# Gate and value of a gated feed-forward layer: plain products in 512-token blocks, and Strassen's seven products of halves

## The chip, the cores and the metric

The kernel runs on one core of a Trainium2 chip. The metric is the device time of one execution in microseconds (us). The engines named below are TensorE (PE in the rows; PEld is its weight load), VectorE (DVE), ScalarE (ACT), GpSimd (POOL) and SyncE (SP), which issues every transfer here. SBUF is the on-chip memory of 128 partitions, PSUM the eight accumulator banks of 128 x 512 fp32 into which TensorE writes, DRAM the memory off the core.

## The reference

```python
# attention: 4 batches, 8 heads, 576 tokens, head 64, causal window 128
x = attention(q, k, v)                 # 2304 tokens x 512
h = np.maximum(x @ w_in, 0)            # moe1: 512 -> 2048
x = (h * h) @ w_out                    #       2048 -> 512
gate = 1 / (1 + np.exp(-(x @ w_gate))) # moe2: 512 -> 1536
val  = x @ w_val                       #       512 -> 1536
out  = (gate * val) @ w_out2           #       1536 -> 512
```

The weights arrive as 64-bit floats. All matrix products are of fp32 accuracy.

## The kernel before

Each weight tile of 128 x 512 is read from DRAM as 64-bit words, turned into fp32 by one operation of ScalarE and four of VectorE (`weight`, L422 to L432), and split into a rounded high part `wh` and the remainder `wl` (the copy at L335, the subtraction at L332). Activations are split likewise. A product then takes three matmuls: high by high, high by low, low by high.

The program has three stages that overlap. Attention and moe1 go through 8 chunks of 256 or 320 tokens; an H step is one of the 16 column tiles of `w_in`, a Y step the matching row tile of `w_out`, and attention for later chunks is laid between the steps. moe1's result goes to DRAM (`yscr`). moe2 works in one block of 256 tokens and four of 512. For each of twelve column tiles `f`, `gv` makes gate and value, each in one PSUM bank (`pg`, `pv`) by 4 x 3 matmuls over the four 128-row pieces of the contraction (L885 to L887), with no break on the bank. Then ScalarE takes the sigmoid (L896), VectorE multiplies (L898), and the product is split into `asp` (`asp5` in the blocks of 512; L335, L332). One tile later `o_step` adds it onto the four output banks, three matmuls of 512 columns each (L915 to L917).

The order of the instructions on every engine is fixed when the program is built. `op` records an operation with the engines that may do it, its keys read and written, and a priority; `Plan.schedule` then replays the program with a cost for each operation (VectorE's is `dve_ns`, L37: 68 + n/0.96 ns for n elements) and lets each engine take the ready operation of lowest priority whose buffers fit. `GROUP` says from which group of SBUF or PSUM slots a buffer comes, `SIZE` how many a group has, `CAP` how many of a kind may be held at once. moe2's weights are loaded, unpacked and split beside the end of moe1 and the first block (`WB`), and stay in SBUF.

Of the kernel before, what the change touches and what calls it, by code (L numbers as in the profile page):

```python
# [287 lines left out]
def attention_moe_moe2_kernel(ctx: ExitStack, tc, q, k, v, w_in, w_out1, w_gate, w_val, w_out2, out):  # L288
# [169 lines left out]
    def attend(u, due, long):  # L458
# [13 lines left out]
        for src, t0, nt, a0 in ((q, u.q0, nq, 0), (k, u.k0, nk, 2 * nq)):
            a = t0 * 128
            r = min(128, (S - a) // nt)
            if pq:
                t = turned[a0] = new("nq" if a0 == 0 else "nk", [128, nt, 2, 64], F32, early)
                op({"SP": 630}, lambda e, t=t, src=src, a=a, nt=nt, r=r: nc.sync.dma_start(
                    out=t()[0:r], in_=src[u.b, h0:h0 + 2, a:a + r * nt, :].rearrange("h (p j) d -> p j h d", j=nt)),
                   w=[t], prio=pl, data=364 * nt)
                continue  # L480

            def load(e, src=src, nt=nt, a0=a0, a=a, r=r):
                nc.sync.dma_start(
                    out=nat()[0:r, a0:a0 + 2 * nt].rearrange("p (h j) d -> p h (j d)", h=2),
                    in_=src[u.b, h0:h0 + 2, a:a + r * nt, :].rearrange("h (p j) d -> p h (j d)", j=nt))

            op({"SP": 475}, load, w=[(nat, a0)], prio=pl, data=182 * nt)
# [24 lines left out]
        if pq:  # L512

            qs, ks = new("qs", [128, 256], F32, early), new("ks", [128, 384], F32, early)
            parts = ((qs, nq, vq, 0), (ks, nk, vk, 2 * nq))
            banks = [new("tq", [128, 512], F32, early)] * 2 if kind == "c" else [new(kd, [128, 512], F32, early) for kd in ("tq", "tk")]
            c0s = (0, nqc if kind == "c" else 0)

            def turn(e, which):
                for z in which:  # L520
                    _, nt, v_, a0 = parts[z]
                    for j in range(nt):
                        nc.tensor.transpose(banks[z]()[:, c0s[z] + j * v_:c0s[z] + (j + 1) * v_],
                                            turned[a0]()[0:v_, j].rearrange("p h d -> p (h d)"), C["ident"][0:v_, 0:v_])

            def place(e, z):
                dst, nt, v_, _ = parts[z]
                nc.scalar.activation(
                    out=in_order(dst()[:, :nt * v_], nt), in_=by_tile(banks[z]()[:, c0s[z]:c0s[z] + nt * v_], nt), func=AF.Copy,
                    scale=C["qmul"][:, u.hp:u.hp + 1] if z == 0 else 1.0)  # L530

            for which in ((0, 1),) if kind == "c" else ((0,), (1,)):
                op({"PE": sum(parts[z][1] * 2 * pe_ns(parts[z][2]) for z in which) + (60 if kind == "c" else 0)},
                   lambda e, which=which: turn(e, which), cols=.5, r=[turned[parts[z][3]] for z in which],
                   w=[banks[which[0]]], prio=p(1 + which[0] / 2), also=[parts[z][0] for z in which])
            for z in range(2):
                op({"ACT": act_ns(parts[z][1] * parts[z][2], True) + (94 if z == 0 else 0)}, lambda e, z=z: place(e, z),
                   r=[banks[z]], w=[parts[z][0]], prio=p(1.3 + z / 2))
        else:

            qkn = new("qkn", [128, 10, 2, 64], F32R)
            op({"ACT": act_ns(64 * n)}, copy(lambda: qkn()[:, :n, 0], lambda: nat()[:, :n]), r=qkkeys, w=[(qkn, 0)], prio=p(0))
            op(dve_or_pool(64 * n), minus(lambda: qkn()[:, :n, 1], lambda: nat()[:, :n], lambda: qkn()[:, :n, 0]),
               r=qkkeys + [(qkn, 0)], w=[(qkn, 1)], prio=p(0), port=True)
            qs, qw = new("qs", [128, 2, 256], F32R, early), new("qw", [128, 2, 256], F32R, early)
            if kind == "b":
                ks = [new("ks", [128, 384], F32R, early) for i in range(2)]
                kof = lambda i, c0, c1: ks[i]()[:, c0:c1]
            else:
                ks = [new("ks", [128, 2, 256], F32R, early)] * 2  # L550
                kof = lambda i, c0, c1: ks[i]()[:, i, c0:c1]

            def turn(what, prio, also):
                banks = [new(kd, [128, 512], F32, early) for kd, _, _ in what]

                def go(e):
                    for ps, (_, rows, v) in zip(banks, what):
                        for z, t in enumerate(rows):
                            nc.tensor.transpose(ps()[:, z * v:(z + 1) * v].bitcast(F32R),
                                                qkn()[0:v, t].rearrange("p x d -> p (x d)"), C["identr"][0:v, 0:v])  # L560

                op({"PE": sum(len(rows) * pe_ns(v) for _, rows, v in what) + 54}, go, r=[(qkn, 0), (qkn, 1)], w=banks, prio=prio, also=also)
                return banks

            whole = ("tq", range(2 * nq), 128)
            if kind == "b":
                ps, = turn([whole], p(1), [qs, qw])
                kps = turn([("tk", range(2 * nq + i * nk, 2 * nq + (i + 1) * nk), 128) for i in range(2)], p(2), ks)
            else:
                ps, kps = turn([whole, ("tk", range(2 * nq, n), 128)], p(1), [qs, qw, ks[0]])  # L570
            for i in range(2):
                op({"ACT": act_ns(nqc, True)}, copy(
                    lambda i=i: in_order(qs()[:, i, :nqc], nq), lambda i=i, ps=ps: by_tile(ps()[:, i * nqc:(i + 1) * nqc], nq),
                    qmul[h0 + i]), r=[ps], w=[(qs, i)], prio=p(1.5))
            for i in range(2):
                r_, o_ = slice(64 * i, 64 * i + 64), slice(64 - 64 * i, 128 - 64 * i)
                def swap(e, r_=r_, o_=o_):
                    if e == "ACT":
                        nc.scalar.activation(out=qw()[o_, :, :nqc], in_=qs()[r_, :, :nqc], func=AF.Copy)
                    else:  # L580
                        nc.vector.tensor_copy(qw()[o_, :, :nqc], qs()[r_, :, :nqc])

                op({"DVE": dve_ns(2 * nqc, True)}, swap, r=[(qs, 0), (qs, 1)], w=[(qw, i)], prio=p(2), port=True)
            if kind == "b":
                for i in range(2):
                    op({"ACT": act_ns(nkc, True)}, copy(
                        lambda i=i: in_order(ks[i]()[:, :nkc], nk), lambda i=i: by_tile(kps[i]()[:, :nkc], nk)),
                       r=[kps[i]], w=[(ks[i], i)], prio=p(2))
            else:
                op({"ACT": act_ns(2 * nkc, True)}, copy(  # L590
                    lambda: ks[0]()[:, :, :nkc].rearrange("c h (p j) -> c h j p", j=nk),
                    lambda: kps()[:, :2 * nkc].rearrange("c (h j p) -> c h j p", h=2, j=nk)),
                   r=[kps], w=[(ks[0], 0), (ks[0], 1)], prio=p(2))
# [434 lines left out]
```

## Time and profile before

| what | us |
|---|---|
| median of 3 runs (1014.94 to 1016.01) | 1015.13 |
| the profiled execution | 1015.93 |
| its span, first to last instruction | 1014.2 |
| TensorE busy | 1002.9 |
| ScalarE busy | 462.9 |
| VectorE busy | 442.9 |
| GpSimd busy | 107.9 |

The profile is of one execution and gives each instruction's start and duration. Matmuls are pipelined, so the duration of one is longer than its distance from the next; the distance is the price of a matmul in a row of them. A busy TensorE is not one at its peak. The granted clock is given in parts of full speed.

### The profile page before, as it was taken

To read this page: it belongs to the slowest core of one execution; us is meant where nothing else is said; L and a number is where in the kernel's file an instruction comes from. 1 tells how busy PE (TensorE), PEld (TensorE's weight loads), DVE (VectorE), ACT (ScalarE), POOL (GpSimd) and SP (SyncE) were. 2 spreads that over 40 slices of the span, in tenths; PEclk is the share of its full clock that TensorE was granted. 3 is DMA by queue.
4 is the path that set the end of the run, shared out by engine and by line. 5 is a ranking of instruction groups with operands and counts; after the bars stand their busy time and mean duration, and the time that the engine had idled before them with its cause. 6 is when DMAs were issued, how large, how long until landed. Compare 5 with 4: busy or idle time off the path is not lost.

```text
span 1014.2 us, 16829 instructions
## 1 busy us (share of the span) xinstructions
PE 1002.9 (99%) x6308; PEld 875.0 (86%) x6308; DVE 442.9 (44%) x1248; ACT 462.9 (46%) x1235; POOL 107.9 (11%) x224
## 2 busy tenths in 40 slices
PE   8999999999999999999999999999999999999998
PEld 6699999998998988998999998888888888888886
DVE  6999963344244243246799972112211221111112
ACT  7887875566555465556677552111211221112111
POOL 3513121122021021021000110000000000000000
PEclk9999999999999999999999999999999999999999
DMA  8556562022312113111455540001100110001001
GB/s 229 136 166 181 161 183 56 21 53 53 86 30 55 31 39 71 35 45 42 138 157 167 171 146 22 1 11 32 42 1 10 32 42 1 1 1 42 0 1 42
DMA packets 112594, 69.26 MB, mean 68 GB/s; under 512 B 79488, under 2 KB 104576, under 8 KB 112512
## 3 DMA queue, kind: packets, MB, share of 16 engines
q1 hardware_dynamic: 112512, 68.18, 23.9%
q8 instruction: 50, 0.82, 0.3%
q14 instruction: 32, 0.26, 0.1%
HBM read 58.72 MB, written 9.44 MB: 67 GB/s over the span
## 4 chain that ended last, share of the span: by engine, by line
PE 89%; ACT 3%; DVE 3%; DMA 3%; issue 1%; SPq 0%; ACTq 0%
PE y L811 18%; PE h L774 6%; PE h L776 6%; PE h L775 6%; PE pg L886 5%; PE pv L886 5%; PE o L915 5%; PE pv L887 5%; PE pg L885 5%; PE pv L885 5%; PE o L917 5%; PE o L916 5%; PE pg L887 5%; PE tv L752 3%; PE ts L614 2%; DMA raw<-in_moe_w_in_dram 2%
## 5 line engine op out<-in xcount | busy, mean ns | idle before, releaser
L811 PE MATMUL y<-gs,wh 128*128 128x256 f32 (+1 forms) x1024 | 216.6, 303 | 0.5 <-DVE gs L332 0.4
L811 PEld LDWEIGHTS y<-gs,wh 128*128 128x128 f32 x1024 | 163.1, 189 | 12.1 <-issue 9.3
L898 DVE TENSOR_TENSOR a<-pv,a 128x512 f32<-128x512 f32 (+1 forms) x60 | 38.3, 638 | 292.2 <-PE pv L887 290.9
L774 PE MATMUL h<-x,wh 128*128 128x256 f32 (+1 forms) x512 | 157.6, 308 | 0.4 <-DVE r L786 0.4
L811 PE MATMUL y<-gs,wl 128*128 128x256 f32 (+1 forms) x512 | 151.2, 295 | 0.0
L776 PE MATMUL h<-x,wl 128*128 128x256 f32 (+1 forms) x512 | 151.2, 295 | 0.0
L775 PE MATMUL h<-x,wh 128*128 128x256 f32 (+1 forms) x512 | 151.1, 295 | 0.0
L896 ACT ACTIVATE a<-pg 128x512 f32<-128x512 f32 (+1 forms) x60 | 33.3, 555 | 189.0 <-PE pg L887 188.8
L332 DVE TENSOR_TENSOR gs<-r,gs 128x320 fp32r<-128x320 f32 (+1 forms) x121 | 56.5, 467 | 137.6 <-ACT gs L335 137.0
L774 PEld LDWEIGHTS h<-x,wh 128*128 128x128 f32 x512 | 97.2, 190 | 5.0 <-issue 3.2
L335 ACT ACTIVATE asp<-a 128x512 fp32r<-128x512 f32 (+1 forms) x60 | 35.3, 589 | 144.1 <-DVE a L898 144.0
L775 PEld LDWEIGHTS h<-x,wh 128*128 128x128 f32 x512 | 96.8, 189 | 0.0
L811 PEld LDWEIGHTS y<-gs,wl 128*128 128x128 f32 x512 | 96.6, 189 | 0.0
L776 PEld LDWEIGHTS h<-x,wl 128*128 128x128 f32 x512 | 96.4, 188 | 0.0
L887 PE MATMUL pv<-x,wl 128*128 128x512 f32 (+1 forms) x240 | 89.2, 372 | 0.0
L885 PE MATMUL pv<-x,wh 128*128 128x512 f32 (+1 forms) x240 | 89.1, 371 | 0.0
L885 PE MATMUL pg<-x,wh 128*128 128x512 f32 (+1 forms) x240 | 89.1, 371 | 0.0
L887 PE MATMUL pg<-x,wl 128*128 128x512 f32 (+1 forms) x240 | 89.1, 371 | 0.0
L729 POOL TENSOR_SCALAR_AFFINE_SELECT pt<-pt 128x256 f32<-128x256 f32 (+1 forms) x144 | 65.1, 474 | 223.1 <-ACT pt L723 206.8
L788 ACT ACTIVATE r<-h 128x256 f32<-128x256 f32 (+1 forms) x128 | 51.8, 406 | 78.9 <-PE h L776 75.7
L915 PE MATMUL o<-wh,asp 128*128 128x512 f32 x216 | 85.2, 395 | 0.0
L917 PE MATMUL o<-wh,asp 128*128 128x512 f32 x216 | 85.2, 394 | 0.0
(105 smaller groups left out, 1763.0 us busy)
## 6 DMA issues: line engine op xcount, KB each, us to landing
raw<-in_moe_w_out_dram SPq DMA_DIRECT2D x28, 512.0 KB, 3.6
raw<-in_moe_w_in_dram SPq DMA_DIRECT2D x16, 512.0 KB, 4.8
raw<-in_moe_w_gate_dram SPq DMA_DIRECT2D x12, 512.0 KB, 3.6
raw<-in_moe_w_val_dram SPq DMA_DIRECT2D x12, 512.0 KB, 3.6
ysg<-yscr SPq DMA_DIRECT2D x18, 256.0 KB, 2.7
out_dram<-ob SPq DMA_DIRECT2D x18, 256.0 KB, 2.0
nq<-in_q_dram SPq DMA_DIRECT2D x32, 128.0 KB, 3.0
yscr<-ys SPq DMA_DIRECT2D x32, 128.0 KB, 1.8
```

What stands on the lines that cost most here:

```text
L332: return lambda e: eng(e).tensor_tensor(out=out(), in0=a(), in1=b(), op=ALU.subtract)
L729: op({"POOL": pool_sel(2 * cols)}, lambda e: nc.gpsimd.affine_select(out=pt_of(what, j), in_=pt_of("own", j), pattern=[[0, 2], [1 if mine ...
L774: nc.tensor.matmul(ps()[:, :N], w[0]()[:, c], x()[:, 0, cc, :N], start=cc == 0, stop=False)
L775: nc.tensor.matmul(ps()[:, :N], w[0]()[:, c], x()[:, 1, cc, :N], start=False, stop=False)
L776: nc.tensor.matmul(ps()[:, :N], w[1]()[:, c], x()[:, 0, cc, :N], start=False, stop=cc == CC - 1)
L788: op({"ACT": act_ns(N, True)}, lambda e: nc.scalar.activation(out=g()[:, :N], in_=ps()[:, :N], func=AF.Relu), r=[ps], w=[g], prio=ep, also ...
L811: nc.tensor.matmul(y()[:, c0:c0 + N], w[a]()[:, c], gs()[:, b, :N], start=f == 0 and p == 0 and n != 1, stop=f == F1 - 1 and p == 2, skip_ ...
L885: nc.tensor.matmul(ps()[:, :NB], w[0]()[:, c], x(0, cc), start=cc == 0, stop=False)
L886: nc.tensor.matmul(ps()[:, :NB], w[0]()[:, c], x(1, cc), start=False, stop=False)
L887: nc.tensor.matmul(ps()[:, :NB], w[1]()[:, c], x(0, cc), start=False, stop=cc == CC - 1)
L915: nc.tensor.matmul(o(), asp()[:, 0, c], w[0](), start=f == 0, stop=False)
L917: nc.tensor.matmul(o(), asp()[:, 1, c], w[0](), start=False, stop=f == F2 - 1)
```

## The change

Gate and value in the four blocks of 512 tokens are made by Strassen's scheme. For a pair of column tiles `f`, `f + 1` of one kind, the weight is a 2 x 2 arrangement of halves (rows of the contraction by column tiles), and so is the block (halves of the tokens by halves of the contraction). Instead of eight products of halves there are seven, P1 to P7, of sums and differences of halves, each of 2 x 3 matmuls of 256 columns. A unit (one kind, one pair) uses two PSUM banks, `pa` and `pd`. P1 goes onto `pa` and ScalarE copies it out; P6, P5 and P3 are added onto the same bank, with copies between. P2 goes onto `pd`, VectorE adds it to a copy; P7 restarts `pd`, VectorE adds that, and P4 is added onto it. The output tiles, four quarters each, come together in SBUF buffers `cg`. `ORDER` spreads the seven products and the four output steps over a unit by priority.

```diff
+    ORDER = ["P1", "P2", "o0", "P6", "o1", "P7", "P5", "o2", "P3", "o3", "P4"]
+    at_unit = {u: 3.0 * i / len(ORDER) for i, u in enumerate(ORDER)}
+    def gv_strassen(n, kind, f, e0):
+        (gh, gl), (_, v2), (t2, t3, t1, t4) = W[kind, f], W[kind, f + 1], TW.pop((n, kind, f))
+        pa, pd = new("pa", [128, 512], F32), new("pd", [128, 512], F32)
...
+            op({"PE": 6 * pe_ns(256)}, go, r=wk + [(bh, ih), (bl, il)] + ([] if start else [ps]), w=[ps], prio=e0 + at_unit[name])
...
+        product("P1", pa, True)
+        product("P2", pd, True)
+        keep(0, 0, pr)
+        add(0, 0, pr)
+        product("P6", pa, False)
+        product("P7", pd, True)
+        keep(0, 1, pr)
+        product("P5", pa, False)
+        keep(1, 1, pr)
+        add(1, 1, pr)
+        product("P3", pa, False)
+        product("P4", pd, False)
+        add(0, 1, pr)
```

`keep` is a copy of 256 columns by ScalarE, `add` an addition of 256 columns by VectorE. For a gate unit three sigmoids follow (256, 256 and 512 elements), for a value unit three multiplications by the gate and two splits. `xb` makes the seven operands of a block's tokens: four quarters are loaded, four sums or differences made, and seven splits.

The weights' operands are made once. During moe1, from chunk 2 to the beginning of chunk 7, `prepare` loads the two tiles of a pair, unpacks them, forms four differences of halves (`tt`), splits all, and stores four pieces of 512 KB in DRAM (`wscr`); `prepare_out` does the same without differences for each output tile. `weight2` reads the plain split weights back once, and `sums` reads the four split differences (`st2`) of a unit in every block.

```diff
+    first, last = begin[2], begin[NC - 1]
+    for f in range(0, F2, 2):
+        jobs += [(prepare, "gate", f), (prepare, "val", f), (prepare_out, f), (prepare_out, f + 1)]
+    for i, (fn, *a) in enumerate(jobs):
+        fn(*a, first + (last - first) * (i + 1) / len(jobs))
...
+            weight2(kind, f, endA + j * 0.7 - 18)
...
+                sums(n, kind, f0, e1 - 9)
+                gv_strassen(n, kind, f0, e1)
...
+    def put(u, p, k, prio):
+        op({"SP": 475}, lambda e: nc.sync.dma_start(
+            out=scr(u, k, 2).rearrange("(k p) c -> p k c", p=128), in_=p().bitcast(F32)),
...
+        for i, x, y, rk in ((1, B[12], B[11], [tg, tw]), (3, B[22], B[12], [tw]), (2, B[22], at_t[1], [tw, (tb, 1)]), (4, B[21], at_t[2], [tg, (ta, 2)])):
+            op(dve_or_pool(256), minus(at_t[i], x, y), r=rk, w=[(tb if i in (1, 4) else ta, i)], prio=prio + .5, port=True)
...
-    CAP = {"raw": 3, "nat": 2, "nq": 2, "nk": 2, "qs": 1, "qw": 1, "ks": 1, "wt": 6, "vs": 3, "st": 4, "pt": 2, "t": 3,
-           "h": 2, "y": 4, "pg": 2, "pv": 2, "o": 4, "ob": 4, "ob5": 2, "ysg": 2, "a5": 2, "asp5": 2}
+    CAP = {"raw": 3, "nq": 1, "nk": 1, "qs": 1, "ks": 1, "wt": 6, "vs": 3, "st": 4, "pt": 2, "t": 3,
+           "h": 2, "y": 4, "pg": 2, "pv": 2, "o": 4, "pa": 2, "pd": 2, "ob": 2, "ysg": 2, "raw2": 2, "pp": 1, "xp": 2,
+           "tg": 1, "tw": 1, "tt": 2, "st2": 6, "xf": 6, "cg": 4, "ah": 3, "al": 3}
...
-    o_step(*prev, endA + 3.0 * F2 * nblk)
+    o_step(nblk - 1, F2 - 2, endA + 3.0 * F2 * nblk, False)
+    o_step(nblk - 1, F2 - 1, endA + 3.0 * F2 * nblk, False)
```

The queries and keys of an attention unit now have one buffer each (`nq`, `nk`), and a branch of attention that was never taken is gone. Since both tiles of a pair come at once, the output step for a tile is recorded two tiles later instead of one, and those of the last pair both at the end.

How the order on the engines moves is shown at three places. First TensorE in a block of 512 tokens, before: the end of a value tile and the beginning of the output step; `pv` is the value's bank, `o` an output bank, `x` and `xs` the tokens, a number tells one buffer from another, and the brackets name the engines for which an instruction waits.

```order
L885 MATMUL pv_9976<-x_9365,wh_6789 128x512
L886 MATMUL pv_9976<-xs_9407,wh_6789 128x512
L887 MATMUL pv_9976<-x_9365,wl_6800 128x512
L915 MATMUL o_9995<-wh_6711,asp5_9951 128x512 [waits Activation_49]
L916 MATMUL o_9995<-wl_6723,asp5_9951 128x512
L917 MATMUL o_9995<-wh_6711,asp5_9951 128x512 [waits Pool_49]
L915 MATMUL o_10000<-wh_6711,asp5_9951 128x512 [waits DVE_49]
L916 MATMUL o_10000<-wl_6723,asp5_9951 128x512
```

And after, within a pair of units, where L936 is the product of `gv_strassen` and L1030 to L1032 the output step; `pa_10350` and `pd_10360` are the gate's two banks, `pa_10370` one of the value's, `st2` and `ah`, `al` the differences and the split result.

```order
L936 MATMUL pa_10370<-x_9473,wl_7924 128x256
L936 MATMUL pa_10350<-x_9473,st2_10262 128x256 [waits DMAHW4_49,Activation_49]
L936 MATMUL pa_10350<-x_9500,st2_10262 128x256
L936 MATMUL pa_10350<-x_9473,st2_10262 128x256 x2
L936 MATMUL pa_10350<-x_9500,st2_10262 128x256
L936 MATMUL pa_10350<-x_9473,st2_10262 128x256
L936 MATMUL pd_10360<-x_9500,st2_10292 128x256 [waits DMAHW5_49,DVE_49]
L936 MATMUL pd_10360<-x_9500,st2_10292 128x256 x5
L1030 MATMUL o_9765<-wh_7823,ah_10378 128x512 [waits Activation_49]
L1031 MATMUL o_9765<-wl_7826,ah_10378 128x512
L1032 MATMUL o_9765<-wh_7823,al_10388 128x512 [waits DVE_49]
L1030 MATMUL o_9771<-wh_7823,ah_10378 128x512
```

Where twelve matmuls of 512 columns stood on one bank without a wait inside, P6 and P7 of the gate now stand between two pieces of other banks, and each waits for the reading of its bank and for a load.

Second, TensorE at the end of the program, before, where `asp5_10402` and `asp5_10446` are the split results of the last two tiles; twelve matmuls of the first stand between the last value product and the first of the second.

```order
L886 MATMUL pv_10424<-xs_9407,wh_8103 128x512
L887 MATMUL pv_10424<-x_9365,wl_8109 128x512
L915 MATMUL o_9995<-wh_8021,asp5_10402 128x512 [waits Activation_49]
L916 MATMUL o_9995<-wl_8032,asp5_10402 128x512
L917 MATMUL o_9995<-wh_8021,asp5_10402 128x512 [waits DVE_49]
L915 MATMUL o_10000<-wh_8021,asp5_10402 128x512
...
L915 MATMUL o_9995<-wh_8161,asp5_10446 128x512 [waits Activation_49]
L916 MATMUL o_9995<-wl_8166,asp5_10446 128x512
L917 MATMUL o_9995<-wh_8161,asp5_10446 128x512 [waits DVE_49]
```

And after, where `ah_12479`, `al_12483` and `ah_12481`, `al_12485` are the two results of the last pair.

```order
L936 MATMUL pd_12419<-xp_11585,st2_12383 128x256 [waits DMAHW7_49,DVE_49]
L936 MATMUL pd_12419<-xp_11585,st2_12383 128x256 x5
L1030 MATMUL o_11744<-wh_7943,ah_12479 128x512 [waits Activation_49]
L1031 MATMUL o_11744<-wl_7953,ah_12479 128x512
L1032 MATMUL o_11744<-wh_7943,al_12483 128x512 [waits DVE_49]
L1030 MATMUL o_11744<-wh_8056,ah_12481 128x512 [waits Activation_49]
L1031 MATMUL o_11744<-wl_8063,ah_12481 128x512
L1032 MATMUL o_11744<-wh_8056,al_12485 128x512 [waits DVE_49]
L1030 MATMUL o_11750<-wh_7943,ah_12479 128x512
```

No matmul is left between the last product, P4 on `pd_12419`, and the output step that needs its result; 24 matmuls follow.

Third, VectorE in moe1, beside an H step (`r`, `gs`) and an attention unit (`ts`, `st`, `sm`), before:

```order
L668 RECIPROCAL sm<-sm 128x2
L676 TENSOR_TENSOR st<-st,sm 128x256
L666 TENSOR_SCALAR sm<-sm 128x2
L668 RECIPROCAL sm<-sm 128x2
L825 COPY ys<-y 128x256
L332 TENSOR_TENSOR gs<-r,gs 128x320
L786 TENSOR_TENSOR r<-h,r 128x320
L332 TENSOR_TENSOR gs<-r,gs 128x320
L641 COPY_PREDICATED ts<-msk,ts 128x2x128 x2
L653 ISA st,sm<-ts,rel 128x128
L653 ISA sm 128x1
```

And after, where `tw` and `tg` are the two weight tiles of a pair that are unpacked and `tt` their differences:

```order
L838 COPY ys<-y 128x256
L467 SCALAR_TENSOR_TENSOR tw<-raw_4176,tw 128x512
L679 TENSOR_SCALAR sm<-sm 128x2
L799 TENSOR_TENSOR r<-h,r 128x320
L681 RECIPROCAL sm<-sm 128x2
L666 ISA st,sm<-ts,rel 128x128
L666 ISA sm 128x1
L335 TENSOR_TENSOR tt<-tw,tg 128x256
L799 TENSOR_TENSOR r<-h,r 128x320
L335 TENSOR_TENSOR tt<-tw,tt 128x256
L335 TENSOR_TENSOR gs<-r,gs 128x320
```

Between the same instructions of moe1 and attention there are now a merge of an unpacked weight (L467) and differences of halves (L335 with `tt`).

## Rows read from the trace of the kernel before

**Rows 1.** The page: busy time, the chain's shares; and the view of cores.

```profile
PE 1002.9 (99%) x6308; PEld 875.0 (86%) x6308; DVE 442.9 (44%) x1248; ACT 462.9 (46%) x1235; POOL 107.9 (11%) x224
...
PE 89%; ACT 3%; DVE 3%; DMA 3%; issue 1%; SPq 0%; ACTq 0%
...
core 0: 1014.2 us, clock 0.997
```

**Rows 2.** Waits of TensorE: total us, times, longest; all eight.

```profile
PE warm L984 <- DVE identr L379: 1.8, 1, 1.8
PE tq L523 <- DMA nq<-in_q_dram: 1.5, 1, 1.5
PE tp L719 <- POOL st L676: 1.5, 2, 1.2
PE tp L719 <- ACT st L674: 0.9, 1, 0.9
PE ts L614 <- ACT ks L528: 0.8, 1, 0.8
PE h L774 <- DVE r L786: 0.4, 1, 0.4
PE y L811 <- DVE gs L332: 0.4, 1, 0.4
PE tk L523 <- ACT ks L528: 0.2, 1, 0.2
```

**Rows 3.** Windows: stretch, its us, PE PEld DVE ACT POOL, PEclk, DMA, GB/s.

```profile
25.00:100.00 75.00, 71.68 (x582) 63.09 (x579) 71.56 (x223) 60.56 (x186) 26.57 (x35) 0.98 0.58 164
180.00:500.00 320.00, 320.00 (x2440) 288.07 (x2439) 129.43 (x499) 186.73 (x574) 44.92 (x122) 1.00 0.20 50
500.00:560.00 60.00, 60.00 (x413) 59.98 (x412) 56.30 (x108) 44.27 (x91) 2.75 (x2) 1.00 0.57 177
...
800.00:900.00 100.00, 100.00 (x432) 80.94 (x431) 19.62 (x29) 18.00 (x30) 1.29 (x1) 1.00 0.04 16
```

**Rows 4.** Timeline of TensorE, block of 256 tokens: start, us, instruction.

```profile
556.87 0.28 PE L885 MATMUL pg<-x,wh 128*128 128x256 f32 x1
...
562.90 0.28 PE L885 MATMUL pv<-x,wh 128*128 128x256 f32 x1
...
564.32 0.39 PE L915 MATMUL o<-wh,asp 128*128 128x512 f32 x1
...
565.71 0.28 PE L885 MATMUL pg<-x,wh 128*128 128x256 f32 x1
...
568.53 0.39 PE L915 MATMUL o<-wh,asp 128*128 128x512 f32 x1
```

**Rows 5.** Timeline, a tile of a 512-token block; brackets: idle before, releaser.

```profile
701.40 0.39 PE L885 MATMUL pv<-x,wh 128*128 128x512 f32 x1
701.61 0.60 ACT L896 ACTIVATE a<-pg 128x512 f32<-128x512 f32 x1 [4.16 <-PE pg L887]
704.19 0.39 PE L915 MATMUL o<-wh,asp 128*128 128x512 f32 x1
704.45 0.69 DVE L898 TENSOR_TENSOR a<-pv,a 128x512 f32<-128x512 f32 x1 [6.28 <-PE pv L887]
705.18 0.63 ACT L335 ACTIVATE asp<-a 128x512 fp32r<-128x512 f32 x1 [2.98 <-DVE a L898]
```

**Rows 6.** Groups, shapes apart: count, busy us, ns of one, idle before.

```profile
L429 DVE SCALAR_TENSOR_TENSOR wt<-raw,wt 128x512 int32<-128x512 int32 x68 | 49.8, 734 | 0.6
L432 DVE SCALAR_TENSOR_TENSOR wt<-raw,wt 128x512 int32<-128x512 int32 x68 | 46.7, 691 | 0.2
L332 DVE TENSOR_TENSOR wl<-wt,wh 128x512 fp32r<-128x512 f32 x56 | 38.5, 695 | 3.4 <-ACT wh L335 3.2
L332 DVE TENSOR_TENSOR asp<-a,asp 128x512 fp32r<-128x512 f32 x46 | 31.9, 692 | 30.8 <-ACT asp L335 30.8
L426 DVE TENSOR_SCALAR wt<-wt 128x512 int32<-128x512 int32 x68 | 29.7, 437 | 0.6
L424 DVE TENSOR_SCALAR wt<-wt 128x512 f32<-128x512 f32 x68 | 29.2, 430 | 7.0 <-ACT wt L422 7.0
L898 DVE TENSOR_TENSOR a<-pv,a 128x256 f32<-128x256 f32 x12 | 5.1, 424 | 6.1 <-PE pv L887 4.8 <-ACT wh L335 0.8 <-issue 0.5
L896 ACT ACTIVATE a<-pg 128x256 f32<-128x256 f32 x12 | 4.6, 384 | 6.7 <-PE pg L887 6.6
```

**Rows 7.** The page, DMA issues: count, KB each, median us to landing.

```profile
ysg<-yscr SPq DMA_DIRECT2D x18, 256.0 KB, 2.7
```

**Rows 8.** Timeline, the last matmul of the program.

```profile
1010.08 0.39 PE L917 MATMUL o<-wh,asp 128*128 128x512 f32 x1
```

More of the change, by code (lines that the diff above doesn't have):

```diff
@@ new lines, in fetch, with weight2 @@
+    def fetch(kind, u, k, prio, after=()):
+        b = new(kind, [128, 512], F32R)
+        b.late = True
+        op({"SP": 475}, lambda e: nc.sync.dma_start(out=b().bitcast(F32), in_=scr(u, k)), r=[("scr", u, k)] + list(after), w=[b], prio=prio, data=728)
+        return b
+    def weight2(kind, f, prio):
+        if kind == "out2":
+            W[kind, f] = fetch("wh", (kind, f), GH, prio), fetch("wl", (kind, f), GL, prio)
+        elif f % 2 == 0:
+            W[kind, f] = fetch("wh", (kind, f), GH, prio), fetch("wl", (kind, f), GL, prio)
+        else:
+            W[kind, f] = fetch("v1", (kind, f - 1), V1, prio), fetch("v2", (kind, f - 1), V2, prio)
@@ L474, in attend @@
             r = min(128, (S - a) // nt)
[L475 to L487, printed above, removed]
+            t = turned[a0] = new("nq" if a0 == 0 else "nk", [128, nt, 2, 64], F32, early)
+            op({"SP": 630}, lambda e, t=t, src=src, a=a, nt=nt, r=r: nc.sync.dma_start(
+                out=t()[0:r], in_=src[u.b, h0:h0 + 2, a:a + r * nt, :].rearrange("h (p j) d -> p j h d", j=nt)),
+               w=[t], prio=pl, data=364 * nt)
         a = u.k0 * 128
@@ L507, in attend @@
             vkeys += [(vn, "v", "pad"), (vn, "v", 2)]
-        qkkeys = [(nat, 0), (nat, 2 * nq)]
         vq, vk = (128, 128) if kind != "c" else (S - 512, (S - 384) // 2)
         nqc, nkc = nq * vq, nk * vk
[L512 to L593, printed above, removed]
@@ new lines, in attend, with turn @@
+        qs, ks = new("qs", [128, 256], F32, early), new("ks", [128, 384], F32, early)
+        parts = ((qs, nq, vq, 0), (ks, nk, vk, 2 * nq))
+        banks = [new("tq", [128, 512], F32, early)] * 2 if kind == "c" else [new(kd, [128, 512], F32, early) for kd in ("tq", "tk")]
+        c0s = (0, nqc if kind == "c" else 0)
+        def turn(e, which):
+            for z in which:
+                _, nt, v_, a0 = parts[z]
+                for j in range(nt):
+                    nc.tensor.transpose(banks[z]()[:, c0s[z] + j * v_:c0s[z] + (j + 1) * v_],
+                                        turned[a0]()[0:v_, j].rearrange("p h d -> p (h d)"), C["ident"][0:v_, 0:v_])
@@ new lines, in place @@
+        def place(e, z):
+            dst, nt, v_, _ = parts[z]
+            nc.scalar.activation(
+                out=in_order(dst()[:, :nt * v_], nt), in_=by_tile(banks[z]()[:, c0s[z]:c0s[z] + nt * v_], nt), func=AF.Copy,
+                scale=C["qmul"][:, u.hp:u.hp + 1] if z == 0 else 1.0)
+        for which in ((0, 1),) if kind == "c" else ((0,), (1,)):
+            op({"PE": sum(parts[z][1] * 2 * pe_ns(parts[z][2]) for z in which) + (60 if kind == "c" else 0)},
+               lambda e, which=which: turn(e, which), cols=.5, r=[turned[parts[z][3]] for z in which],
+               w=[banks[which[0]]], prio=p(1 + which[0] / 2), also=[parts[z][0] for z in which])
@@ L596, in attend @@
+        for z in range(2):
+            op({"ACT": act_ns(parts[z][1] * parts[z][2], True) + (94 if z == 0 else 0)}, lambda e, z=z: place(e, z),
+               r=[banks[z]], w=[parts[z][0]], prio=p(1.3 + z / 2))
         st = new("st", [128, 4, 128], F32, early)
```

284 lines of the change are left out of this document (208 added, 76 removed).

## The prediction

> **What bounds the kernel now.** I read the page's busy times first, then the list of waits, then stretches of 50 to 100 us, and last single instructions. TensorE is busy 99% of the span, at a mean granted clock of 0.997, the upper level of 2.4 GHz, and 89% of the chain that ended last is TensorE [rows 1]. Busy time alone does not show that it works at its pace, so I looked at what it waited for: eight waits in the whole run, 1.8 us the longest, 7.4 us together [rows 2]. In moe2 there is no idle time, and the pace is steady: a 512-token block of 432 matmuls takes 100 us, 0.2315 us per matmul of 512 columns [rows 3]. There VectorE and ScalarE are busy 20% and 18%. So in moe2 only TensorE counts, and time is to be had by giving it fewer columns. In moe1, from 180 to 500 us, VectorE is busy 129 of 320 us; from 500 to 560 us, where moe2's weights are unpacked, 56 of 60, and TensorE has no idle time there [rows 3].
>
> **What goes on TensorE.** A block has twelve column tiles each of gate and value, 24 x 12 matmuls of 512 columns, and 144 for the output. After the change two tiles of one kind and two halves of the tokens are seven products of six matmuls of 256 columns: 12 x 7 x 6 = 504 per block, and the 144 stay. The price of a 256-column matmul with a weight load of its own is in the trace, in the block of 256 tokens: 24 of them from 565.71 to 568.53 us, 0.1175 us each; the twelve from 562.90 to 564.32 us, at 0.1183, are the dearer end; six of 512 columns between took 1.39 us [rows 4]. I take 0.1178. New block: 504 x 0.1178 + 144 x 0.2315 = 59.4 + 33.3 = 92.7 us. Old: 432 x 0.2315 = 100.0 us. That is 7.3 us per block and 29.1 us for four; with 0.1183 it is 28.2, with 0.1175 it is 29.8. The first block keeps its products.
>
> **Hand-overs inside a unit, new.** A unit of seven products now uses two PSUM banks, and five of the products are added onto a bank that ScalarE or VectorE must read first. Nothing in the old trace waits like this, so I bound it. Chain for ScalarE: it starts 0.21 us after TensorE's next slot (701.40 to 701.61) [rows 5], copies 256 columns in 0.384 us [rows 6], and a follower on another engine starts 0.04 us after an end (705.14 to 705.18) [rows 5]: 0.64 us. For VectorE 0.26 + 0.424 + 0.04 = 0.72 us [rows 5, 6]. In the new order of TensorE at least two other pieces (a product, 6 x 0.1178 = 0.71 us, or three output matmuls, 0.69 us) stand between a product and the next on its bank, 1.4 us of cover, because gate's and value's units are interleaved and the output step is spread over them. So each hand-over has some 0.7 us to spare: one 512-element instruction in front (0.63 on ScalarE, 0.69 on VectorE [rows 6]) eats it and a second one doesn't fit. Load on these engines in a pair of units, 14 x 0.707 + 8 x 0.695 = 15.5 us of TensorE: on VectorE nine to ten operations of 256 or 512 elements, about 5.4 us; on ScalarE about 5.0 us; at a block's start 7 splits and 4 sums more. Two queues a third full seldom have two long jobs in front. Bounds: 0, and 0.3 us at a tenth of 240 hand-overs, 7 us; I take 0, the value of the output's own hand-over in the old moe2, which never waited.
>
> **The end, new.** Before, the last output step but one covers the hand-over of the last gate and value. After the change both units of the last pair end together, and all 24 remaining output matmuls need their result. From TensorE's last product [rows 5, 6]: 0.26, add 0.424, 0.04, multiplication 0.69, 0.04, rounding copy 0.63, 0.04: 2.1 us idle; the third matmul waits for the low half (0.04 + 0.69, less two matmuls of 0.23), 0.3 us more. +2.4 us. What follows the start of the last matmul, at 1010.08 [rows 8], keeps its 1014.2 - 1010.08 = 4.1 us.
>
> **Weights from DRAM.** The sums of weights are read again for every block: 48 x 256 KB = 12.6 MB per 92.7 us, 136 GB/s. From 500 to 560 us the queues moved 177 GB/s at a share of 0.57 [rows 3], so this is a share of 0.44. A 256 KB load landed in 2.7 us [rows 7]; in the new order each such load goes into a buffer that is freed at least 12 us of TensorE's work before the load's first use. The reads of the split weights for the first block (72 of 256 KB, 18.9 MB) replace 36 of 512 KB, and each stands over 50 us of TensorE's work ahead. Hidden: 0. What it costs if that cover is gone is rival 3.
>
> **Preparation, moved and added.** 36 tiles are unpacked during chunks 2 to 6 instead of beside chunk 7 and the first block. VectorE, for each a clamp, a shift and two merges: 36 x (0.430 + 0.437 + 0.734 + 0.691) = 82.5 us, 60 splits x 0.695 = 41.7, and 48 differences of 256 elements x 0.424 = 20.4, by the nearest row, a multiplication of that size [rows 6]: 145 us. Some of the last two kinds go to GpSimd; its durations for them stand in no row, so I count all on VectorE. (129 + 145)/320 = 86% of VectorE in a stretch where attention also runs. What it takes away after 500 us gains nothing, as no wait stands there. DMA gets 31.5 MB of writes and 18.9 MB of reads: 157 GB/s over 320 us on top of 50 at a share of 0.20 [rows 3], to about 0.7; q and k of a unit now have one buffer, so their loads start later, but a unit of attention is due eight steps of twelve matmuls (8 x 12 x 0.1178, 11 us and more) before its chunk. Bounds for the new waits: from 500 to 560 us VectorE was 94% busy and TensorE lost 0; from 25 to 100 us it was 95% busy with attention beside it, and TensorE's busy time fell short by 3.3 of 75 us [rows 3], which over 320 us is 14. A load of 86% is below both and nearer to the first; I take 2 us. The 36 loads moved there and 60 new stores all go through SP's one queue, and a store waits there for its split; q, k and v of the next units queue behind it, with the same 11 us to spare.
>
> **Sum.** -29.1 + 2.4 + 0 + 0 + 2 = -24.7 us. The profiled execution took 1015.93 us, 1014.2 of it the span: 991.2. The median of the runs is 1015.13, 0.8 lower: **990.4 us**.
>
> **A rule that speaks against the change.** By the rows two matmuls of 256 columns take 2 x 0.1178 = 0.2356 us against 0.2315 for one of 512 [rows 3, 4], 2% dearer per column; that is in the sum. The Trainium skill ("Perfetto Trace Analysis", section Matmuls) calls larger matmuls more efficient, and the trace agrees, by these 2%. The same section wants independent groups to rotate through different PSUM banks, so that one is read beside the next one's matmuls; here a group is read and then continued on its own bank. No row of before shows such a group; what it does if the reading is not covered is rival 1.
>
> **Rivals.**
> 1. *Hand-overs are exposed.* 48 units have five each, 240. From 0.11 us on average they eat the whole 26.7 us, and beyond that the kernel is slower than before. With half a chain exposed (0.3 us) they cost 72 us: 990 + 72 = 1062; with 0.15 us, 1026. For it: there are only two banks of either kind, queues are served in their order, and the order was laid out with 601 ns for a 512-element operation of VectorE (L37) where the trace has 692 [rows 6]. Against it: 1.4 us of cover on a chain of 0.7, and queues at a third. 6%.
> 2. *Moe1 slows down.* VectorE at 86% with two-buffer preparation in front of attention and of moe1's low halves: up to the bound of 14 us, 990 + 12 = 1002. For it: the rows from 25 to 100 us, and SP's queue. Against it: the stretch from 500 to 560 us. 18%.
> 3. *The loads bind.* If a unit's four loads of 2.7 us landed one after another, 10.8 us against 7.7, the four blocks would grow by 48 x 3.1 = 149 us: 1139. Several are in flight at once by the order, so 2%.
> 4. *Less is saved:* the 256-column matmul runs at 0.1183 and a tenth of the hand-overs costs 0.3 us: 990 + 1 + 7 = 998. 10%.
> The forecast itself, 985 to 996, has 64%.
>
> **How the numbers follow.** The sum with 0.1175, no loss in moe1 and no idle end is 990.4 - 0.7 - 2 - 2.4 = 985.3, and I start a little under it; 1004 takes in rivals 2 and 4. That leaves out rivals 1 and 3 and little else, so 984 to 1004. 0.2% is 2 us, about what a measurement of this kernel can tell. Faster: the forecast and rivals 2 and 4, 0.92. Rival 1's 6% are split by its price: 0.02 near its point of decision, the same; the rest with rival 3, slower, 0.06.
>
> **What will show it.** Blocks of about 92.7 us from the first matmul of one to that of the next; 504 matmuls of 256 columns in each, 0.118 us apart. No row of TensorE waiting for ScalarE or VectorE at the product's line, or only short ones at a block's start. One idle time of about 2.4 us some 10 us before the end. VectorE near 85% between 180 and 500 us, and the first moe2 matmul at 557 to 563 us (556.9 before [rows 4]). Wrong if the blocks take over 95 us, or if moe2 starts after 570 us.

## The result and the profile after

| | median us | runs | ratio to before, 95% interval |
|---|---|---|---|
| before | 1015.57 (1014.94 to 1016.02) | 4 | |
| after | 992.35 (991.54 to 994.08) | 4 | 0.9774 [0.9757, 0.9791] |

The kernel is 23.2 us faster; 24.7 were predicted, and 992.35 lies in the range. The profiled execution took 992.02 us, its span 990.3, 23.9 less than before. Busy times and the chain, in the page's columns as in [rows 1]:

```profile
PE 974.1 (98%) x7172; PEld 895.9 (90%) x7172; DVE 546.0 (55%) x1489; ACT 529.0 (53%) x1430; POOL 144.8 (15%) x259
...
PE 91%; ACT 3%; DVE 3%; DMA 2%; issue 0%; SPq 0%; ACTq 0%; DVEq 0%
```

TensorE has 864 matmuls more and is busy 28.8 us less. The list of its waits, longest first, answers to [rows 2]:

```profile
PE tq L608 <- DMA nq<-in_q_dram: 2.5, 2, 2.1
PE o L1030 <- ACT ah L338: 2.0, 1, 2.0
...
PE o L1032 <- DVE asp L335: 0.2, 1, 0.2
```

No row names L936, the line of the products: of 240 hand-overs none shows. The one new long wait is L1030, the end. A short new one is L1032: at 611.25 us, in the first block of 512 tokens, the output step of the small block's last tile waits for a low half. The windows, columns as in [rows 3]:

```profile
180.00:500.00 320.00, 319.67 (x2445) 288.32 (x2444) 212.13 (x666) 212.72 (x629) 79.52 (x149) 1.00 0.61 182
500.00:560.00 60.00, 60.00 (x413) 60.00 (x413) 17.84 (x33) 30.60 (x65) 1.29 (x1) 1.00 0.93 331
720.00:820.00 100.00, 100.00 (x697) 93.19 (x696) 38.31 (x76) 36.44 (x83) 4.47 (x4) 1.00 0.55 165
```

In the 512-token blocks VectorE's work doubles (19.6 to 38.3 of 100 us) and the queues go from a share of 0.04 to 0.55, while TensorE still has no idle time. Where the blocks begin is read from TensorE's timeline (start, us, instruction): the first matmul of chunk 2, of moe2, of the four blocks (in the third one also the first of an output step, 796.64), and the last one.

```profile
150.68 0.28 PE L787 MATMUL h<-x,wh 128*128 128x256 f32 x1
...
557.77 0.28 PE L1003 MATMUL pg<-x,wh 128*128 128x256 f32 x1
...
609.00 0.40 PE L936 MATMUL pa<-x,wh 128*128 128x256 f32 x2
...
698.49 0.40 PE L936 MATMUL pa<-x,wh 128*128 128x256 f32 x2
...
791.67 0.40 PE L936 MATMUL pa<-x,wh 128*128 128x256 f32 x2
...
796.64 0.40 PE L1030 MATMUL o<-wh,ah 128*128 128x512 f32 x1
...
884.87 0.40 PE L936 MATMUL pa<-x,wh 128*128 128x256 f32 x2
...
985.66 0.40 PE L1032 MATMUL o<-wh,al 128*128 128x512 f32 x1
```

The same marks in the kernel before (its moe2 began at 556.87 [rows 4]):

```profile
149.32 0.28 PE L774 MATMUL h<-x,wh 128*128 128x256 f32 x1
...
608.04 0.39 PE L885 MATMUL pg<-x,wh 128*128 128x512 f32 x1
...
807.11 0.40 PE L885 MATMUL pg<-x,wh 128*128 128x512 f32 x1
...
907.46 0.40 PE L885 MATMUL pg<-x,wh 128*128 128x512 f32 x1
```

A middle block takes 791.67 to 884.87, 93.20 us; before, 807.11 to 907.46, 100.35. The four blocks up to the start of the last matmul took 1010.08 - 608.04 = 402.04 us and now take 376.66. That is 25.38 us, more than the whole gain; the 1.0 us by which the blocks begin later and 0.5 us behind the last matmul go off it. The end in the timeline, with the idle time before an instruction and its releaser in brackets:

```profile
977.15 0.86 PE L936 MATMUL pd<-xp,st 128*128 128x256 f32 x6
...
978.05 0.42 DVE L950 TENSOR_TENSOR cg<-pd,cg 128x256 f32<-128x256 f32 x1 [0.28 <-PE pd L936]
978.51 0.69 DVE L980 TENSOR_TENSOR cg<-cg 128x512 f32<-128x512 f32 x1
979.30 1.15 ACT L338 ACTIVATE ah<-cg 128x512 fp32r<-128x512 f32 x2 [3.67 <-DVE cg L980]
...
979.98 0.50 PE L1030 MATMUL o<-wh,ah 128*128 128x512 f32 x1 [1.96 <-ACT ah L338]
980.32 0.40 PE L1031 MATMUL o<-wl,ah 128*128 128x512 f32 x1
980.71 0.50 PE L1032 MATMUL o<-wh,al 128*128 128x512 f32 x1
981.04 0.39 PE L1030 MATMUL o<-wh,ah 128*128 128x512 f32 x1
...
986.30 0.38 ACT L338 ACTIVATE ob<-o 128x256 f32<-128x256 f32 x1 [1.00 <-DMA out_dram<-ob]
```

Addition, multiplication and rounding copy stand one behind the other between the last product and the output step. Counted from its start with six matmuls of 0.118 us, the last product ends at 977.86, so TensorE stands for 2.12 us; the next three matmuls come 0.11, 0.16 and 0.10 us late. The last copy of the output waits for a transfer, which it did not before.

### The profile page after: what moved, and what is told of

The parts are those of the page before. It is cut to its first block, busy times and chain, and to the rows that moved or that the text cites. A ratio compares the mean times of both kernels' runs of the same rounds, so it can differ in the third digit from the quotient of the medians.

```text
span 990.3 us, 20102 instructions
## 1 busy us (share of the span) xinstructions
PE 974.1 (98%) x7172; PEld 895.9 (90%) x7172; DVE 546.0 (55%) x1489; ACT 529.0 (53%) x1430; POOL 144.8 (15%) x259
## 4 chain that ended last, share of the span: by engine, by line
PE 91%; ACT 3%; DVE 3%; DMA 2%; issue 0%; SPq 0%; ACTq 0%; DVEq 0%
PE y L824 20%; PE pa L936 14%; PE pd L936 10%; PE h L787 7%; PE h L788 6%; PE h L789 6%; PE o L1032 5%; PE o L1030 5%; PE o L1031 5%; PE tv L765 3%; PE ts L643 2%; PE tp L732 1%; PE tq L608 1%; DMA raw<-in_moe_w_in_dram 1%; ACT st L673 1%; PE ts L636 1%
## 5 line engine op out<-in xcount | busy, mean ns | idle before, releaser
L950 DVE TENSOR_TENSOR cg<-pd,cg 128x256 f32<-128x256 f32 x144 | 60.6, 424 | 193.7 <-ACT cg L338 127.0
L338 ACT ACTIVATE cg<-pa 128x256 f32<-128x256 f32 x144 | 52.6, 383 | 182.6 <-PE pa L936 175.1
L335 DVE TENSOR_TENSOR gs<-r,gs 128x256 fp32r<-128x256 f32 (+1 forms) x121 | 55.8, 461 | 79.8 <-ACT gs L338 79.4
L936 PE MATMUL pa<-x,st 128*128 128x256 f32 x576 | 83.9, 281 | 0.0
L936 PEld LDWEIGHTS pa<-x,st 128*128 128x128 f32 x576 | 78.1, 189 | 3.9
L1030 PE MATMUL o<-wh,ah 128*128 128x512 f32 x192 | 75.9, 395 | 2.0 <-ACT ah L338 2.0
L1031 PE MATMUL o<-wl,ah 128*128 128x512 f32 x192 | 75.8, 395 | 0.0
L1032 PE MATMUL o<-wh,al 128*128 128x512 f32 x192 | 75.8, 395 | 0.0
L673 ACT ACTIVATE st<-st,sm 128x128 f32<-128x128 f32 x144 | 56.6, 399 | 14.7 <-DVE sm L666 14.3
L338 ACT ACTIVATE gs<-r 128x256 fp32r<-128x256 f32 (+1 forms) x128 | 56.3, 442 | 4.5 <-PE y L824 1.6
```

What stands on the lines that cost most here:

```text
L338: return lambda e: nc.scalar.activation(out=out(), in_=in_(), func=AF.Copy, scale=scale)
L673: op({"ACT": 386}, lambda e, x=x: nc.scalar.activation(out=st()[:, x, :], in_=st()[:, x, :], func=AF.Exp, bias=sm()[:, x:x + 1], scale=-1. ...
L936: nc.tensor.matmul(ps()[:, :256], w()[:, c], x, start=start and cc == 0 and i == 0, stop=cc == 1 and i == 2, skip_group_check=True)
L950: op({"DVE": dve_ns(256)}, lambda e: nc.vector.tensor_tensor(out=half(i, j)(), in0=D(), in1=half(i, j)(), op=ALU.add), r=[pd, (c[i], j)], ...
L1030: nc.tensor.matmul(o(), ah()[:, c], w[0](), start=f == 0, stop=False)
L1031: nc.tensor.matmul(o(), ah()[:, c], w[1](), start=False, stop=False)
```

## The experiments

All are edits of the changed kernel unless said otherwise; ratios are to the kernel before on the same chip.

**e1, no cover.** Each product and each output step gets a common key, so that they keep the order in which they are recorded, and the products are recorded bank by bank.

```diff
-            op({"PE": 6 * pe_ns(256)}, go, ..., w=[ps], prio=e0 + at_unit[name])
+            op({"PE": 6 * pe_ns(256)}, go, ..., w=[ps, ("seq",)], prio=e0 + at_unit[name])
```

> TensorE's products of a unit stand bank by bank (P1, P6, P5, P3, then P2, P7, P4, then the four output steps), in this order and with nothing between, so that every hand-over is exposed. Theory A (the gain rests on cover; chain of 0.64 us for ScalarE, 0.72 us for VectorE, as in the prediction): 48 units x (3 x 0.64 + 2 x 0.72) = 161 us more, about 1153 us, with idle times of 0.6 to 0.75 us before each added product. Rival B (a hand-over is short, 0.3 us or less, and would be hidden in any order): at most 48 x 5 x 0.3 = 72 us more, 1064 us or less. If it is longer, 1 us, then 1232 us.

1179.35 us, ratio 1.1617 [1.1594, 1.1641]. The list of waits has 239 of the 240 hand-overs:

```profile
PE pa L936 <- ACT cg L338: 69.3, 143, 0.8
PE pd L936 <- DVE cg L950: 58.7, 96, 1.8
```

One unit in the timeline:

```profile
747.17 0.97 PE L936 MATMUL pa<-x,st 128*128 128x256 f32 x6 [0.47 <-ACT cg L338]
748.24 0.38 ACT L338 ACTIVATE cg<-pa 128x256 f32<-128x256 f32 x1 [1.12 <-PE pa L936]
748.67 0.97 PE L936 MATMUL pa<-xp,v 128*128 128x256 f32 x6 [0.53 <-ACT cg L338]
...
751.80 0.97 PE L936 MATMUL pd<-x,st 128*128 128x256 f32 x6 [1.45 <-DVE cg L950]
752.88 0.42 DVE L950 TENSOR_TENSOR cg<-pd,cg 128x256 f32<-128x256 f32 x1 [1.13 <-PE pd L936]
753.36 0.98 PE L936 MATMUL pd<-xp,st 128*128 128x256 f32 x6 [0.59 <-DVE cg L950]
```

Two added products behind one another start 751.80 and 753.36, 1.56 us apart, where six slots are 0.71: 0.85 us for VectorE's hand-over. For ScalarE's it is 0.79 (747.17 to 748.67). (The 1.45 us before 751.80 are longer, since VectorE was still at work on the next block's tokens.) Of each, 0.10 us lies inside the product: the six matmuls took 0.97 us instead of 0.87. A block took 141.4 us (744.38 to 885.82), 48.2 more, 4.0 per unit; 3 x 0.79 + 2 x 0.85 = 4.1. So the chains of 0.64 and 0.72 us were right to 0.05, and rival B falls: order alone is worth 187 us here. The expectation was 26 us too low (1153), since it lacked the 0.10 us at each of 240 places.

**e2, one pair of banks.**

```diff
-           ... "pa": 2, "pd": 2, ...
+           ... "pa": 1, "pd": 1, ...
```

> One bank pa and one bank pd instead of two of each. The gate's unit then has P1, P2, P6, P7, P5 with one product (0.71 us) between a product and the next on its bank; the value's unit keeps two pieces by the output steps. Theory A: 24 gate units x 3 hand-overs against a chain of 0.64 to 0.72 us, 0 to 0.1 us each, so 0 to 7 us more: 993 to 1000 us, some with waits for ScalarE or VectorE. Theory of queues (the operations in front eat what is spare, 0.35 us on average): 25 us more, 1017 us. Rival B: no change, 992 us.

997.34 us, ratio 0.9825 [0.9811, 0.984]: 5.0 us over the changed kernel. The list of waits has one row at the products:

```profile
PE pa L936 <- ACT cg L338: 1.6, 3, 0.6
```

With one product (0.71 us) of cover most hand-overs just fit, and the loss is within the 0 to 7 us expected. Most of it is too small for the list: 23 times a matmul of a product onto `pd` comes about 0.10 us late. The queues do not add 0.35 us to each.

**e3, preparation alone.** Blocks of 512 tokens with plain products, their tokens loaded and split as before, and the output step one tile later as before; preparation, stores and first reads as in the changed kernel.

```diff
-                sums(n, kind, f0, e1 - 9)
-                gv_strassen(n, kind, f0, e1)
...
+            gv(n, f, e1)
```

> The preparation in moe1, the stores and the first reads stay as in the changed kernel; the blocks of 512 tokens make gate and value by plain products as before, so the sums of weights are made and never read. Theory A (preparation nearly hidden: moe2 started 0.9 us later in the profile): 1016 to 1017 us, 0.9 us over the kernel before. Rival C (the preparation costs more and the blocks give more): 1019 us or over.

1017.3 us, ratio 1.0023 [1.0013, 1.0034], 1.9 us over before. But the profile puts the loss elsewhere than the expectation did:

```profile
147.68 0.28 PE L787 MATMUL h<-x,wh 128*128 128x256 f32 x1
...
555.10 0.28 PE L976 MATMUL pg<-x,wh 128*128 128x256 f32 x1
...
1008.27 0.40 PE L1008 MATMUL o<-wh,asp 128*128 128x512 f32 x1
...
1009.62 0.38 ACT L338 ACTIVATE ob<-o 128x256 f32<-128x256 f32 x1 [1.93 <-DMA out_dram<-ob]
```

From chunk 2 to moe2 it took 407.42 us; before 556.87 - 149.32 = 407.55, after 557.77 - 150.68 = 407.09. Preparation in moe1 cost nothing. What is lost lies behind the last matmul: 1014.6 - 1008.27 = 6.3 us of span instead of 4.1. Most of it is the output's two buffers instead of four: the third output copy on ScalarE waits 1.93 us for a transfer, the last one starts 2.05 us after the last matmul, and in the kernel before it started 0.42 us after it (1010.50).

And the 0.9 us by which moe2 began later in the changed kernel is scatter of the first 150 us: chunk 2 began at 147.68 here and at 151.22 in e7, with the same order on every engine up to there. In seven profiles with that order up to moe2 (the changed kernel, e1, e2, e3, e5, e7, e9) moe2 began between 555.10 and 558.75 us; before, in its one profile, at 556.87. A part of the scatter goes with the granted clock. The stretch from 40 to 60 us, the changed kernel first and then e3 (columns as in [rows 3]; the clock is the third number from the end):

```profile
40.00:60.00 20.00, 18.21 (x147) 14.43 (x146) 18.80 (x71) 15.62 (x53) 7.06 (x14) 0.91 0.51 149
...
40.00:60.00 20.00, 18.90 (x165) 15.69 (x161) 19.68 (x71) 16.69 (x57) 7.02 (x12) 1.00 0.48 136
```

In e7 it was 0.83 there.

**e4, unpacking twice.** `f64_to_f32` is called a second time on the same words.

> Each of moe2's 36 weight tiles is unpacked twice in a row from the same words, with the same result: 36 x 2.29 = 82 us more for VectorE, so 212 + about 74 = 286 of the 320 us from 180 to 500, 89%, the load that the prediction assumed. Theory A (VectorE has room until it is nearly full): 0 to 3 us more, 992 to 996 us. Rival 2 of the prediction (attention and moe1 wait for a full VectorE): up to 14 us more, 1006 us.

997.09 us, ratio 0.9825 [0.9809, 0.9842]: 4.7 us more, between the two. The windows:

```profile
180.00:500.00 320.00, 318.00 (x2421) 285.56 (x2420) 244.74 (x731) 225.44 (x652) 78.12 (x148) 1.00 0.55 169
500.00:560.00 60.00, 57.45 (x387) 56.52 (x386) 38.72 (x73) 31.94 (x68) 2.44 (x2) 1.00 0.94 328
```

VectorE did not reach 89% but 76%: the work stretched, and a part of it fell behind 500 us (38.7 us of VectorE instead of 17.8). There TensorE lost 2.6 us, waiting for low halves of moe1 (1.6 and 0.8 us at L826), and 2.0 us before. The run does not test the load that it was meant to; it shows that preparation which overruns into the last chunk costs. Another 1.4 us of what this profile lost lie at the end of the program, where the granted clock fell (under e7), and have nothing to do with the preparation.

**e5, reads twice.** Each read of `st2` is issued a second time.

> Each read of a sum of weights from DRAM is issued twice in a row into the same buffer: 384 reads instead of 192, about 294 GB/s instead of 158 in a block of 512 tokens, a share of the queues of about 1.0 instead of 0.53 (from 520 to 540 us they ran 395 GB/s at 1.05 while TensorE was busy 20.00 of 20 us). Theory A (the reads stand 12 us and more ahead, and the queues have room): blocks keep 93.2 us, 992 to 995 us. Rival 3 (the loads bind when they come late): blocks grow by 5 us or more each, 1012 us or over, with TensorE waiting for the reads.

999.53 us, ratio 0.9834 [0.9801, 0.9867], 7.2 us more. A window of 100 us, as above from 720 us on:

```profile
720.00:820.00 100.00, 96.59 (x661) 88.67 (x660) 37.93 (x74) 34.12 (x78) 5.78 (x5) 1.00 0.86 282
```

At 282 GB/s and a share of 0.86 TensorE has idle time. The list of waits has four for the reads at the products, 2.6 us in all, and five more there that it puts down to ScalarE's copies, 2.5 us. The first three blocks grew by 0.8, 3.6 and 3.8 us (90.3, 96.75, 97.0), the last one not at all. Less than rival 3 asked, more than theory A allowed.

But the edit did two things. Both reads of a pair write the same buffer, so the second (L527) waits in SyncE's queue until the first has landed, and all later transfers stand behind it. The list of SyncE's waits has it first:

```profile
SPq L527 <- DMA st<-wscr: 182.4, 161, 3.2
```

So late reads cost what rival 3 said they would, waits at the products; whether they came late by the doubled load or by a queue that stood for 182 us is not shown.

**e6, two buffers for queries and keys,** `"nq": 2, "nk": 2`.

> Queries and keys of an attention unit have two buffers each again, as before the change. If the 1 to 2 us that moe1 lost came from their loads starting later: moe2 starts 1 to 2 us after the point that the run with one buffer would give, so 990.5 to 991.5 us. If they came from the preparation's work on VectorE and ScalarE: no change, 992 us.

1010.1 us, ratio 0.995 [0.9935, 0.9965]: 17.8 us more, which neither theory had. Three windows:

```profile
350.00:360.00 10.00, 6.80 (x60) 4.08 (x54) 7.91 (x25) 7.08 (x24) 3.78 (x10) 0.94 0.72 196
360.00:370.00 10.00, 7.16 (x39) 6.04 (x38) 3.59 (x19) 4.41 (x16) 2.82 (x4) 0.55 0.72 207
260.00:370.00 110.00, 101.13 (x708) 87.13 (x705) 68.06 (x220) 70.80 (x209) 22.05 (x50) 0.92 0.58 172
```

Ahead of chunk 5, which began at 365.79 instead of 352.11, TensorE had only attention to do and waited for its loads and for GpSimd. It was busy 6.80 of 10 us, and then the granted clock fell to 0.55, close to the lower level of 1.2 GHz. From 260 to 370 us it was idle for 8.9 us, and a mean granted clock of 0.92 over 110 us is, as an estimate, as much again.

**e8, the same with 15 slots held back for attention instead of 13** (`keep = 15 - sum(...)`).

> As e6 (two buffers each for queries and keys), and the SBUF slots that are held back from early weight reads as long as attention lasts are 15 instead of 13, two more for the two new buffers. Theory A (in e6 the weight reads took the room of attention's buffers, its units came late and in a bunch ahead of chunks 4 and 5, and TensorE waited there at a lower granted clock): the bunches go, 990 to 993 us, granted clock 1.00 from 180 to 500 us. Theory B (two buffers put the queries' and keys' loads behind the stores in the queue of SyncE, whatever the room): the loss stays, 1005 us or over.

991.17 us, ratio 0.9759 [0.9742, 0.9775]. The first two windows again:

```profile
350.00:360.00 10.00, 10.00 (x72) 9.34 (x71) 8.65 (x38) 8.08 (x28) 3.46 (x5) 1.00 0.68 217
360.00:370.00 10.00, 10.00 (x77) 8.60 (x75) 4.37 (x12) 6.06 (x18) 2.28 (x6) 1.00 0.56 166
```

With room held back for the two new buffers the loss is gone, as theory A had it: it was a matter of room, not of the queue of SyncE. The 1.2 us to the changed kernel are within the runs' scatter, so two buffers bring nothing that these runs show.

**e9, four buffers for the sums instead of six,** `"st2": 4`.

> Four buffers instead of six for the sums of weights, so a read can start later by two products or more, about a third of its lead of 12 us. Theory A (3.0 us from issue to landing against a lead of about 8 us): no change, 992 us, blocks of 93.2 us. Rival 3 (the lead was needed): waits of TensorE for the reads at the products, 996 us or over.

990.56 us, ratio 0.976 [0.9738, 0.9782]: no loss, no wait for a read at a product. A shorter lead is enough.

**e7, the end.** The output step of tile 9 is held back, tile 11's result is split and used before tile 10's, its low halves come after its high ones, and the last block's output has four buffers.

```diff
-    o_step(nblk - 1, F2 - 2, endA + 3.0 * F2 * nblk, False)
+    o_step(nblk - 1, F2 - 3, endA + 3.0 * F2 * nblk - 1, False)
     o_step(nblk - 1, F2 - 1, endA + 3.0 * F2 * nblk, False)
+    o_step(nblk - 1, F2 - 2, endA + 3.0 * F2 * nblk + 1, False)
...
+                for z in range(2):
+                    op({"PE": (2 - z) * pe_ns(512)}, lambda e, go=go, z=z: go(e, low=z), r=[akeys[z], w[0], w[1]], w=[o],
...
-                ob = new("ob", [128, DM], F32)
+                ob = new("obz" if n == nblk - 1 else "ob", [128, DM], F32)
```

> The end alone is changed: the output step of the last but two tile is held back, the last tile's result (ready one product earlier) is split and used before the last but one's, its four low-half matmuls come after its eight high-half ones, and the last block's output buffers are four instead of two. Theory A (2.1 us idle for the result of the last pair, 0.4 us for an output buffer): idle time before the last output steps goes to 0.2 us or less and the time after the last matmul back to 4.1 us: 2.5 us less, about 989.8 us. Rival (the pieces held back were cover for hand-overs in the last pair, which now wait): 991 to 992 us with waits at L936 near 970 us.

988.48 us, ratio 0.9736 [0.9722, 0.9751], the lowest of all. The end in the timeline:

```profile
977.38 0.87 PE L936 MATMUL pd<-xp,st 128*128 128x256 f32 x6
...
978.08 0.40 PE L1032 MATMUL o<-wh,ah 128*128 128x512 f32 x1
978.10 0.63 ACT L338 ACTIVATE ah<-cg 128x512 fp32r<-128x512 f32 x1 [2.24 <-DVE cg L976]
...
978.78 0.49 PE L1032 MATMUL o<-wh,ah 128*128 128x512 f32 x1
...
984.19 0.39 PE L1035 MATMUL o<-wh,al 128*128 128x512 f32 x1
```

The held-back step fills 978.08 to 978.78, and the idle time of 2.1 us is gone; from the last block's first matmul (885.79) to its last it took 98.40 us instead of 100.79. Behind the last matmul it is 988.6 - 984.19 = 4.4 us instead of 4.6. Together 2.6 us, as theory A had it. The median gained 3.9, and the granted clock may be a part of the rest. In four of the seven profiles with the changed kernel's end (e4, e6, e8, e9) it fell to its lower level, 0.50 to 0.52 over 3 us, right after TensorE had stood for 2.1 us; in e9:

```profile
978.00:981.00 3.00, 3.00 (x8) 2.15 (x7) 1.02 (x3) 0.48 (x2) 0.00 (x0) 0.50 0.00 0
```

There it took 9.24 to 9.41 us from the last matmul of the last product to the last matmul of the program; in the other three (the changed kernel, e2, e5) 7.88 to 7.94. So this end takes 1.4 us more in some executions. In e7's profile, which has no gap, the clock stays at 1.00 there; its other runs left no timeline, so for the median this is not shown.

## Why the prediction was right

**Columns: right, 0.7 us too much.** Predicted 29.1 us for four blocks (its own prices give 29.2: 4 x (288 x 0.2315 - 504 x 0.1178)). Measured 25.38, and added back 2.5 of idle time at the end and 0.5 at the first block's L1032: 28.4. A block takes 93.20 us instead of 92.7, and took 100.24 on the mean of two (706.98 to 907.46) instead of 100.0. The matmul of 256 columns ran at the dearer end, 0.1183 us (42 of them from 791.67 to 796.64), with which the prediction had 28.2. The wait at L1032, 0.37 us and 0.10 at the matmul behind it, stood in no term. (The eight waits of [rows 2] add up to 7.5 us, not 7.4; nothing hangs on it.)

**Hand-overs: right.** Predicted 0, measured 0 at L936. e1 shows that each would cost 0.79 to 0.85 us without cover and e2 that one product of cover is nearly enough; the order gives two. This was the term on which the sign hung: 240 uncovered hand-overs turn 23 us faster into 164 us slower. Rival 1 priced half a chain, 0.3 us and 1062 us; a whole one, with the 0.10 us behind it, made it 1179. The Trainium skill ("Perfetto Trace Analysis", section Matmuls) wants independent groups to rotate through PSUM banks, so that the reading of one lies beside the matmuls of the next; the trace agrees, with 187 us between e1 and the changed kernel, and shows that a group which is read and continued on its bank pays nothing as long as others stand between.

**The end: right.** Predicted 2.4 us; measured 2.12 + 0.11 + 0.16 + 0.10 = 2.5 in this profile. That the clock can fall behind it, for 1.4 us more (under e7), was not foreseen.

**Behind the last matmul: missed.** The prediction kept its 4.1 us; it is 4.6. About 0.2 of it come from `CAP`, which gives the output two buffers: the row with `out_dram<-ob` as releaser shows it, e3 shows 1.6 us of the same, and e7 gets 0.2 back with four. The other 0.3 lie behind the last copy, in e7 too, and their cause is not shown.

**Preparation: smaller than predicted.** 2 us were taken, with bounds of 0 and 14; measured is 0 from chunk 2 to moe2 (407.09 against 407.55, and 407.42 in e3). VectorE was busy 212 of 320 us, 66%, where the prediction had 86%, and the queues at 0.61, where it had about 0.7. Of its 145 us of preparation 108 fell into that stretch, 17 before it and 7 behind it, the rest went to GpSimd; and of VectorE's other work there 25 us are gone too, while GpSimd was busy 34.6 us more than before. Rival 2 does not hold at this load, and no run reached 86% there. e4 shows one way to its cost: work that is late for the last chunk. The rival's other leg, loads of queries, came true in e6, by room in SBUF rather than by VectorE.

**Reads: right in size of the effect, low in the load.** Predicted a share of 0.44 at 136 GB/s; measured 0.55 at 165, since a block's tokens and output, 1 MB each, move too. Nothing waits; e9 shows lead to spare, and e5 that reads which come late do make TensorE wait.

In the profile the parts add up: 25.4 us gained in the blocks and 0.4 from chunk 2 to the blocks, 0.5 lost behind the last matmul and 1.4 by a later chunk 2, so 23.9; the medians give 23.2. That the forecast came so near is luck in part. What it had too much (0.7 in the columns) and did not have (0.5 at L1032, 0.5 behind the last matmul) is cancelled by the 2 us for a preparation that cost nothing, and the 1.4 us by which chunk 2 began later in this profile are scatter that no term held.

## What to carry to other kernels

A chain through another engine between two matmul groups on one bank costs nothing where other groups of about twice its length stand between (1.4 us on 0.7 here), and little where they just equal it (e2); count the pieces in the order and the links of the chain from rows, and test both with one run that forces the worst order. At the end of a program such a chain has no cover by itself: hold back independent work for it, as e7 does. Where buffers of one pool serve two stages, a change of one count can starve the other stage; look at the granted clock there, since a short bunch of waits costs more than the waits.

## What the runs showed of the hardware that was not expected

A product that begins after a wait takes 0.97 us for six matmuls of 256 columns, 0.10 us more than the 0.87 of one that follows without a wait (e1 beside the changed kernel); a hand-over costs that much more than its chain.

In e6 the waits that the list names between 260 and 370 us come to under 9 us, and the kernel lost 17.8. The granted clock was 0.55 from 360 to 370 us, after a stretch in which TensorE was busy 6.80 of 10 us; and 0.85 and 0.81 in the two stretches from 270 to 290, in the first of which it was busy 7.56 of 10 us. So a part of the loss is matmuls that ran at a lower clock after the waits.

The same stands behind a single idle time: at the end of the changed kernel TensorE stands once for 2.1 us, and in four profiles of seven the granted clock right behind it is 0.50 to 0.52 over 3 us (e7's section).
